# Windowed attention with channel mix on one core: the converted weights' bits in PSUM between VectorE's operations, and eight in place of six blocks begun in seven slots

## The chip, the cores and the metric

One core of one Trainium2 chip. The metric is the device time of one execution in microseconds (us); the median of three runs stands for the kernel.

## The reference

Attention with a window of 96 keys and 8 global keys, a bias that falls with distance, and a gated channel mix of its output with the output of the token before:

```python
scores = q @ k.T / 8 + bias, masked            # B = 4, H = 8, S = 768, D = 64
x = (softmax(scores) @ v) as [4, 768, 512]
x_prev = x shifted by one token
xk = mu_k * x + (1 - mu_k) * x_prev
xr = mu_r * x + (1 - mu_r) * x_prev
k = max(xk @ w_k, 0)                           # w_k: 512 x 1024
out = sigmoid(xr @ w_r) * ((k * k) @ w_v)      # w_r: 512 x 512, w_v: 1024 x 512
```

q, k and v are float32, the three weights float64; the output is float32.

## The kernel before

**Tiles and chunks.** The 3072 queries are 24 tiles of 128 (6 for each batch), each with all 8 heads. For a tile, `scores` makes four products s (two heads each), VectorE adds the bias and takes the row maximum (e, L295), ScalarE takes the exponent (L296), VectorE the reciprocal of the sums of four heads (r, L302 and L303), and GpSimd scales the four heads' e by it (L306). `transposes` turns e on TensorE (t, L317) and ScalarE copies it (et, L318). `weighted` makes the products av with v (L334). Two tiles are a chunk of 256 tokens, x, and twelve chunks go through the channel mix: `mix` (GpSimd's or ScalarE's product and VectorE's L358, then hi and lo parts, xk_lo and xr_lo at L360), four products kp of 24 matmuls (L371 to L373 in `three`), their squares kk (L397 to L400), two products z of 12, two products vps of 24, and the output sig. The first seven tiles (NATIVE) multiply plain float32; from tile 7 on queries and keys are split into two float32r parts (qh, ql, kw; L265 and L266).

**Weights.** The float64 weights are 20 blocks of 128x512: 0 to 7 of w_k, 8 to 11 of w_r, 12 to 19 of w_v. `weight_begin` loads block i's words (raw, in the profile w or w64_i; 512 KB), ScalarE takes the high word's absolute value into a (in the profile wa), and a range step follows: for i < 8 on GpSimd (L167), for later blocks on VectorE (L170). Three operations of VectorE put the float32's bits together: shift and mask (L171), sign (L172), low word (L173). ScalarE or GpSimd rounds a to the hi part (L196 is GpSimd's), and `weight_end` subtracts on GpSimd for the lo part (L180). In all VectorE does 3 operations for each of blocks 0 to 7 and 4 for each of the others, 72.

**Buffers.** Blocks 0 to 7 lie in the buffers of the channel mix (f_pool); raw of the others takes one of three buffers t4k, which mixes and raw queries and keys use too; a of the others one of four f2. In PSUM there are eight banks: two for s, two for t, one for av, and three with the tag "f", which the idle products at the start, kp, z and vps share. A buffer of a tag is taken again when the last reader of the tile before it is done.

**What sets the order.** The main loop calls, for each tile and each of its four pairs of heads, the transposes and scores, then `run_ffn` for pieces of an earlier chunk's channel mix (a chunk begins LAG = 3 tiles after its first tile), then `weights_go`, which begins blocks up to a number n of the slot. On top of that the framework's scheduler orders the instructions of each engine by a model of their times, so the order on an engine need not be that of the code, and a changed line can reorder others. The order is fixed when the kernel is built. Each engine works through its own list; SyncE issues the loads in order, each waiting for its buffer.

Of the kernel before, what the change touches and what calls it, by code (L numbers as in the profile page):

```python
# [9 lines left out]
F32 = mybir.dt.float32  # L10
F32R = mybir.dt.float32r
BF16 = mybir.dt.bfloat16
I32 = mybir.dt.int32
U32 = mybir.dt.uint32
AF = mybir.ActivationFunctionType
ALU = mybir.AluOpType
# [3 lines left out]
B, H, S, D = 4, 8, 768, 64  # L20
# [3 lines left out]
NCHUNK = NTILES // 2  # L24
NATIVE = 7  # first tiles, whose scores are plain float32 products
GMAX = 32
LMAX = 97
NEG = -1.0e9
FAR = 1.0e12
HUGE = (1.875 - 2.0**-13) * 2.0**32  # bits 0x4FEFFC00  # L30


@with_exitstack
def tile_biased_attention_channel_mix(ctx: ExitStack, tc: tile.TileContext, qT, kT, v, n_sizes, mu_kr, w_k, w_v, w_r, q_rows, k_rows, v_rows, slopes, out):
    nc = tc.nc
    vec, act, pool, pe = nc.vector, nc.scalar, nc.gpsimd, nc.tensor

    const = ctx.enter_context(tc.tile_pool(name="const", bufs=1))

# [1 line left out]
    sizes_w = const.tile([128, 2, 2], I32, name="sizes_w")  # L41
    nc.sync.dma_start(sizes_w.rearrange("p s w -> p (s w)"), n_sizes.partition_broadcast(128))
    words = const.tile([128, 2, 2], F32, name="words")
    sizes = const.tile([128, 2], F32, name="sizes")
# [15 lines left out]

# [1 line left out]
    wts = {}  # L62
# [17 lines left out]
    ps_f = fast.enter_context(tc.tile_pool(name="ps_f", bufs=3, space=PSUM))  # L80

    # the tensor engine's clock rises with use: products of zeros until the first tile is there
    zeros = const.tile([128, 512], BF16, name="zeros")
# [4 lines left out]

# [1 line left out]
    # The distance; n_local for a key that is only global, which is over any distance of a local key;  # L90
    # FAR or more where masked: such a key's weight is exactly 0.
    pat = const.tile([128, H, 256], BF16, name="pat")
# [9 lines left out]
    ints, flts, local, glo, dist0, dist = (piece() for _ in range(6))  # L102
    ints = ints.bitcast(I32)
    j = flts[:, 224:352]
    # 96 keys before the tile, then the tile's own
    pool.iota(ints[:, 96:224], [[-1, 128]], base=0, channel_multiplier=1)
# [7 lines left out]

    # tile 0
    vec.tensor_scalar(local[:, 96:224], causal, nlf, FAR, op0=ALU.is_ge, op1=ALU.mult)
# [9 lines left out]

    # later tiles: 32 keys from the start, 96 keys before the tile, the tile
    vec.tensor_scalar(local[:, 0:96], flts[:, 0:96], nlf, FAR, op0=ALU.is_ge, op1=ALU.mult)
# [15 lines left out]
    def weight_begin(i):  # L144
        # A float64 weight's words: (sign, 11 exponent bits, 20 bits), (32 bits).
        # a: its first 24 significant bits as a float32; hi: a rounded to float32r; lo: the rest of a.
        name, src, k, c = w_steps[i]
        if name != "k":
            raw = p4k.tile([128, 512, 2], I32, tag="t4k", name=f"w64_{i}")
            a = f2_pool.tile([128, 512], I32, tag="f2", name=f"wa_{i}")  # L150
        elif k < 2:
            both = f_pool.tile([128, 2048], I32, tag=("kk_hi", "kk_lo")[k], name=f"w64_{i}")
            raw = both[:, 0:1024].rearrange("p (n w) -> p n w", w=2)
            a = both[:, 1024:1536]
        else:
            t = "xk" if k == 2 else "xr"
            raw = f_pool.tile([128, 512, 2], I32, tag=t + "_hi", name=f"w64_{i}")
            a = f_pool.tile([128, 512], I32, tag=t + "_lo", name=f"wa_{i}")
        nc.sync.dma_start(raw.rearrange("p n w -> p (n w)"), src[k * 128 : (k + 1) * 128, 2 * c : 2 * c + 1024])
        low, top = raw[:, :, 0], raw[:, :, 1]  # L160
        hi = wts[name][0][:, k, c : c + 512]
        # top's bits as a float32: times 2**-112 (or 2**16, which differs in a bit that the shift drops) moves the float64
        # exponent's bias to the float32's. What float32 cannot hold is bounded: from 2**128 up (by Inf, which stays Inf,
        # or the min) to a large number, under 2**-127 (by underflow or the max) to 0.
        if i < 8:
            act.activation(a.bitcast(F32), top.bitcast(F32), AF.Abs, scale=2.0**111)
            pool.tensor_scalar(a.bitcast(F32), a.bitcast(F32), 2.0**-112, 2.0**-111, op0=ALU.mult, op1=ALU.mult)  # L167
        else:
            act.activation(a.bitcast(F32), top.bitcast(F32), AF.Abs, scale=2.0**16)
            vec.tensor_scalar(a.bitcast(F32), a.bitcast(F32), 2.0, HUGE, op0=ALU.max, op1=ALU.min)  # L170
        vec.tensor_scalar(a, a, 3, 0x7FFFFFF8, op0=ALU.logical_shift_left, op1=ALU.bitwise_and)  # L171
        vec.scalar_tensor_tensor(a, top, -0x80000000, a, op0=ALU.bitwise_and, op1=ALU.bitwise_or)  # L172
        vec.scalar_tensor_tensor(a, low, 29, a, op0=ALU.logical_shift_right, op1=ALU.bitwise_or)  # L173
        (act.copy if i % 4 < 2 else pool_copy)(hi, a.bitcast(F32))
        w_live[i] = a
# [21 lines left out]

# [1 line left out]
    state = {}  # L199
    # the first tiles' queries and keys, with 64 rows of zeros: products of all 128 rows keep the tensor engine's clock up  # L200
    padded = []
# [40 lines left out]
    def global_v(n):  # L242
        # the tile before, now with the 32 first rows in place of its own
        b, t = divmod(n, NT)
        if t >= 2:
            nc.sync.dma_start(state[n - 1]["va"][0:32], v[b, 0:32, :])
# [99 lines left out]

# [1 line left out]
    def mix(xc, xp, tag, tmp_pool, out_pool, on_act=False):  # L348
# [73 lines left out]

# [1 line left out]
    LAG = 3  # tiles from a chunk's first to the start of its channel mix  # L424
    queue = []
# [15 lines left out]
    for step in range(NTILES + 1):  # L441
        if step + 1 < NTILES:
            load_tile(step + 1)
        if step < NTILES:
            load_v(step)
        for hp in range(4):
            if hp == 0 and step > 1:
                for i in range(4):
                    weighted(step - 2, i)
                global_v(step - 1)  # L450
            if step:
                transposes(step - 1, hp)
            if step < NTILES:
                scores(step, hp)
            if hp == 0:
                if step >= LAG and (step - LAG) % 2 == 0:
                    queue.append(ffn((step - LAG) // 2))
                    if len(queue) == 1 and step == LAG:
                        budget[0] = -17.5
            run_ffn(2.5)  # L460
            run_ffn(2.5)
            if hp == 1 and step + 1 < NTILES:
                split_tile(step + 1)
            slot = 4 * step + hp
            n = min(8, 2 + slot * 4 // 3) if slot < 6 else 8 + (slot - 5) * 6 // 7
            weights_go(n, n - 1 if n <= len(w_steps) else n)
# [7 lines left out]

# [1 line left out]
    def wide():  # L476
        with ExitStack() as g:
# [5 lines left out]
            ps_f = g.enter_context(tc.tile_pool(name="g_psf", bufs=3, space=PSUM))  # L483
            xs = dram.tile([B * DM, S], F32, name="xs")

            dist, keep = ([once.tile([128, S], F32, name=f"{n}_{t}") for t in range(NT)] for n in ("dist", "keep"))
# [9 lines left out]
            for t in range(NT):  # L496
                pool.iota(ji, [[-1, S]], base=t * 128, channel_multiplier=1)
                vec.tensor_copy(rel, ji)
                loc = keep[t]
                vec.tensor_scalar(loc, rel, 0.0, None, op0=ALU.is_ge)  # L500
                vec.tensor_scalar(tmp, rel, nlf, None, op0=ALU.is_lt)
                vec.tensor_mul(loc, loc, tmp)
                # only global: n_local; else the distance
                vec.tensor_sub(tmp, glob, loc)
                vec.tensor_scalar(tmp, tmp, 0.0, None, op0=ALU.max)
                vec.tensor_scalar(keep_n, tmp, nlf, None, op0=ALU.mult)
                vec.tensor_scalar(tmp, tmp, -1.0, 1.0, op0=ALU.mult, op1=ALU.add)
                vec.scalar_tensor_tensor(dist[t], rel, -1.0, rel, op0=ALU.mult, op1=ALU.max)
                vec.tensor_mul(dist[t], dist[t], tmp)
                vec.tensor_add(dist[t], dist[t], keep_n)  # L510
                vec.tensor_max(keep[t], loc, glob)
# [68 lines left out]

    # 1 where the short windows do not hold every kept key
    okf = const.tile([128, 2], F32, name="okf")
# [56 lines left out]
```

## Time and profile before

| | |
|---|---|
| median of 3 runs | 526.06 us (525.92 to 526.25) |
| the profiled execution: span, and with what lies around it | 524.1 us, 526.06 us at the median |
| TensorE busy | 495.9 us, 95% of the span |
| VectorE busy | 372.4 us, 71% |
| ScalarE busy | 323.6 us, 62% |
| GpSimd busy | 283.0 us, 54% |
| chain that ended last | PE 80%, DVE 11%, POOL 5% |
| page's TensorE clock | 0.7 to 0.9 of full in parts of the first 65 us, full behind |

PE is TensorE (PEld its weight loads), DVE VectorE, ACT ScalarE, POOL GpSimd, SP SyncE. L12 is line 12 of the kernel. In a row of a timeline the first number is the start, the second the duration in us (from the first's start to the last's end where several are joined: x4); "out<-in" names tiles without their numbers. An instruction's duration can overlap the next one on its engine by its start-up, so the distance of two starts is what an instruction costs in a row of them. Shares over the whole span mix the start-up, in which weights are converted, with the long stretch behind it.

### The profile page before, as it was taken

How to read it: one execution, taken by the hardware profiler on the slowest of the kernel's cores; microseconds unless marked ns; L12 is line 12 of the kernel's file. 1: busy time of each engine (PE TensorE's matmuls, PEld its weight loads, DVE VectorE, ACT ScalarE, POOL GpSimd, SP SyncE). 2: the span in 40 equal slices, each digit the busy share in tenths (PEclk: the TensorE clock that was granted, in tenths of full speed). 3: DMA queues.
4: the chain of work that ended last, by engine and by line, in shares of the span. 5: the costliest groups of instructions: out<-in, count | busy, mean ns of one | idle time of the engine just before them, and what ended most of it. 6: DMA issues, size and time to landing. Idle time of an engine off the chain costs nothing.

```text
span 524.1 us, 9900 instructions
## 1 busy us (share of the span) xinstructions
PE 495.9 (95%) x3466; PEld 427.2 (82%) x3466; DVE 372.4 (71%) x854; ACT 323.6 (62%) x730; POOL 283.0 (54%) x410
## 2 busy tenths in 40 slices
PE   7885888979999999999999999999999999999995
PEld 4563766869898898898898898898898898898984
DVE  6799999987677766767767867767777865535321
ACT  4868585823957856846847757756757667643220
POOL 8799977987355644544547645535547634203000
PEclk9979799999999999999999999999999999999999
DMA  8998268150350530530521431521422210000101
GB/s 197 322 232 198 67 185 188 41 144 20 107 134 6 141 107 5 157 91 8 162 76 38 130 86 34 133 86 59 124 62 66 62 46 26 35 12 2 41 1 44
DMA packets 27304, 48.16 MB, mean 92 GB/s; under 512 B 7216, under 2 KB 13360, under 8 KB 27248
## 3 DMA queue, kind: packets, MB, share of 16 engines
q1 hardware_dynamic: 27104, 47.46, 34.0%
q8 instruction: 29, 0.48, 0.4%
q14 instruction: 27, 0.22, 0.1%
q10 hardware_dynamic: 144, 0.00, 0.0%
HBM read 41.16 MB, written 6.29 MB: 91 GB/s over the span
## 4 chain that ended last, share of the span: by engine, by line
PE 80%; DVE 11%; POOL 5%; issue 3%; DMA 1%; ACT 0%; DVEq 0%; POOLq 0%
PE vps L372 8%; PE vps L373 8%; PE vps L371 8%; PE kp L371 8%; PE kp L373 8%; PE kp L372 8%; PE av L334 7%; PE t L317 6%; PE z L371 4%; PE z L373 4%; PE z L372 4%; PE s L290 3%; PE s L289 3%; POOL e L306 2%; PE s L287 2%
## 5 line engine op out<-in xcount | busy, mean ns | idle before, releaser
L306 POOL TENSOR_SCALAR e<-e,r 128x256 f32<-128x256 f32 (+1 forms) x192 | 106.1, 570 | 137.0 <-DVE r L303 91.9
L371 PE MATMUL kp<-xk_hi,wk_hi 128*128 128x256 f32 x384 | 108.0, 282 | 0.2 <-DVE kk L398 0.2
L373 PE MATMUL kp<-xk_hi,wk_lo 128*128 128x256 f32 x384 | 107.5, 280 | 0.5 <-POOL wk_lo L180 0.5
L372 PE MATMUL kp<-xk_lo,wk_hi 128*128 128x256 f32 x384 | 107.3, 279 | 0.0
L296 ACT ACTIVATE e<-e,nmax 128x256 f32<-128x256 f32 (+1 forms) x192 | 92.6, 484 | 22.0 <-DVE nmax L295 21.0
L295 DVE CUSTOM_DVE_ANT_0 e<-s,pat 128x256 f32<-128x256 f32 (+1 forms) x192 | 69.0, 395 | 31.0 <-PE s L290 21.2
L372 PE MATMUL vps<-wv_lo,kk_hi 128*128 128x512 f32 x192 | 76.0, 396 | 2.6 <-POOL wv_lo L180 2.6
L371 PE MATMUL vps<-wv_hi,kk_hi 128*128 128x512 f32 x192 | 75.9, 395 | 0.4 <-POOL wv_hi L196 0.4
L373 PE MATMUL vps<-wv_hi,kk_lo 128*128 128x512 f32 x192 | 75.8, 395 | 0.0
L371 PEld LDWEIGHTS kp<-xk_hi,wk_hi 128*128 128x128 f32 x384 | 72.9, 190 | 1.2 <-DVE kk L398 0.6
L373 PEld LDWEIGHTS kp<-xk_hi,wk_lo 128*128 128x128 f32 x384 | 72.8, 190 | 0.9 <-POOL wk_lo L180 0.9
L372 PEld LDWEIGHTS kp<-xk_lo,wk_hi 128*128 128x128 f32 x384 | 72.9, 190 | 0.6
L318 ACT COPY et<-t 128x512 f32<-128x512 f32 (+1 forms) x96 | 52.0, 546 | 20.2 <-PE t L317 19.7
L317 PE MATMUL t<-ident,e 128*128 128x128 f32 x352 | 57.5, 280 | 5.7 <-POOL e L306 5.6
L398 DVE TENSOR_TENSOR kk<-kp,kk 128x512 f32<-128x512 f32 x48 | 33.1, 689 | 41.2 <-ACT kk L397 41.0
L317 PEld LDWEIGHTS t<-ident,e 128*128 128x128 f32 x352 | 41.2, 141 | 19.1 <-POOL e L306 9.2
L334 PE MATMUL av<-et,va 128*64 128x128 f32 x704 | 49.4, 284 | 0.6 <-ACT et L318 0.6
L334 PEld LDWEIGHTS av<-et,va 128*64 128x64 f32 x704 | 40.3, 139 | 10.5 <-issue 5.8
L400 DVE TENSOR_TENSOR kk_lo<-kk,kk_hi 128x512 fp32r<-128x512 f32 x48 | 35.3, 735 | 17.4 <-ACT kk_hi L399 17.3
L399 ACT CAST kk_hi<-kk 128x512 fp32r<-128x512 f32 x48 | 29.8, 622 | 25.6 <-DVE kk L398 25.6
L397 ACT ACTIVATE kk<-kp 128x512 f32<-128x512 f32 x48 | 28.3, 590 | 26.7 <-PE kp L373 24.5
L372 PEld LDWEIGHTS vps<-wv_lo,kk_hi 128*128 128x128 f32 x192 | 36.0, 187 | 10.5 <-POOL wv_lo L180 3.1
(103 smaller groups left out, 1051.1 us busy)
## 6 DMA issues: line engine op xcount, KB each, us to landing
kraw<-in_kT_dram SPq DMA_DIRECT2D x36, 256.0 KB, 3.9
qraw<-in_qT_dram SPq DMA_DIRECT2D x34, 256.0 KB, 4.1
va<-in_v_dram SPq DMA_DIRECT2D x24, 256.0 KB, 3.1
out_dram<-sig SPq DMA_DIRECT2D x24, 256.0 KB, 3.5
w<-in_w_k_dram SPq DMA_DIRECT2D x8, 512.0 KB, 9.1
w<-in_w_v_dram SPq DMA_DIRECT2D x8, 512.0 KB, 3.5
kz<-in_kT_dram SPq DMA_DIRECT2D x8, 256.0 KB, 6.7
w<-in_w_r_dram SPq DMA_DIRECT2D x4, 512.0 KB, 9.3
```

What stands on the lines that cost most here:

```text
L295: vec.tensor_tensor_reduce(out=e[:, :w], in0=o, in1=p[:, h, :], op0=ALU.add, op1=ALU.min, scale=-0.125, scalar=3.0e38, accum_out=s["nmax"] ...
L296: act.activation(e[:, :w], e[:, :w], AF.Exp, bias=s["nmax"][:, h : h + 1], scale=-1.0, accum_out=s["sum"][:, h : h + 1])
L306: pool.tensor_scalar(e[:, :w], e[:, :w], r[:, u : u + 1], 1.0, op0=ALU.mult, op1=ALU.mult)
L317: pe.transpose(pt[:, c : c + 128], e[:, k * 128 : (k + 1) * 128], ident)
L318: act.copy(et[:, : 2 * nb * 128], pt[:, : 2 * nb * 128])
L334: pe.matmul(o, vt[:, h * 64 : (h + 1) * 64], et[:, c : c + 128], start=k == 0, stop=k == nb - 1)
L371: pe.matmul(o, sh, mh, start=first, stop=False)
L372: pe.matmul(o, sh, ml, start=False, stop=False)
L373: pe.matmul(o, sl, mh, start=False, stop=last)
L398: vec.tensor_mul(kk, pv, kk)
L399: act.copy(kkh[:, 2 * fp : 2 * fp + 2, :], kk)
L400: vec.tensor_sub(kkl[:, 2 * fp : 2 * fp + 2, :], kk, kkh[:, 2 * fp : 2 * fp + 2, :])
```

## The change

The bits of block i get a tile of their own in PSUM, wb_i, with the tag "f". The range step of the later blocks (L170) writes there, the shift (L171) and the sign (L172) read and write there, and the low word's operation (L173) reads it and writes a in SBUF as before. From slot 6 on, blocks are begun at a rate of 8 in 7 slots, not 6 in 7. One line is added, so from L162 on every line of the code before has a number higher by one in the changed kernel. Comments are taken out, which moves nothing.

```diff
         hi = wts[name][0][:, k, c : c + 512]
+        bits = ps_f.tile([128, 512], I32, name=f"wb_{i}", tag="f")
         if i < 8:
             act.activation(a.bitcast(F32), top.bitcast(F32), AF.Abs, scale=2.0**111)
             pool.tensor_scalar(a.bitcast(F32), a.bitcast(F32), 2.0**-112, 2.0**-111, op0=ALU.mult, op1=ALU.mult)
         else:
             act.activation(a.bitcast(F32), top.bitcast(F32), AF.Abs, scale=2.0**16)
-            vec.tensor_scalar(a.bitcast(F32), a.bitcast(F32), 2.0, HUGE, op0=ALU.max, op1=ALU.min)
-        vec.tensor_scalar(a, a, 3, 0x7FFFFFF8, op0=ALU.logical_shift_left, op1=ALU.bitwise_and)
-        vec.scalar_tensor_tensor(a, top, -0x80000000, a, op0=ALU.bitwise_and, op1=ALU.bitwise_or)
-        vec.scalar_tensor_tensor(a, low, 29, a, op0=ALU.logical_shift_right, op1=ALU.bitwise_or)
+            vec.tensor_scalar(bits.bitcast(F32), a.bitcast(F32), 2.0, HUGE, op0=ALU.max, op1=ALU.min)
+        vec.tensor_scalar(bits, a if i < 8 else bits, 3, 0x7FFFFFF8, op0=ALU.logical_shift_left, op1=ALU.bitwise_and)
+        vec.scalar_tensor_tensor(bits, top, -0x80000000, bits, op0=ALU.bitwise_and, op1=ALU.bitwise_or)
+        vec.scalar_tensor_tensor(a, low, 29, bits, op0=ALU.logical_shift_right, op1=ALU.bitwise_or)
...
             slot = 4 * step + hp
-            n = min(8, 2 + slot * 4 // 3) if slot < 6 else 8 + (slot - 5) * 6 // 7
+            n = min(8, 2 + slot * 4 // 3) if slot < 6 else 8 + (slot - 5) * 8 // 7
```

The scheduler answers with another order. In the rows below an instruction has its line, its operation, what it writes and reads with the tiles' numbers, and its size; t_3_0 is tile 3's first transpose, kp_700 and kp_748 are chunk 0's first product in the one and the other kernel, mix_k and xk_lo of chunk 0 are its mixes.

TensorE, before: where chunk 0's products begin, among the transposes of tile 3.

```order
L334 MATMUL av_2_729<-et_2_3_676,va_2_413 64x128
L317 MATMUL t_3_0_750<-ident_62,e_3_0_582 128x128 x2
L371 MATMUL kp_700<-xk_hi_589,wk_hi_70 128x256
L371 MATMUL kp_783<-xk_hi_589,wk_hi_70 128x256
L317 MATMUL t_3_0_750<-ident_62,e_3_1_585 128x128 x2
L317 MATMUL t_3_1_812<-ident_62,e_3_2_634 128x128 x2
L317 MATMUL t_3_1_812<-ident_62,e_3_3_637 128x128 x2
L372 MATMUL kp_700<-xk_lo_590,wk_hi_70 128x256
```

TensorE, after: where chunk 0's products begin.

```order
L335 MATMUL av_5_1480<-et_5_3_1433,va_5_1021 64x128
L318 MATMUL t_6_3_1642<-ident_62,e_6_6_1442 128x128
L318 MATMUL t_6_3_1642<-ident_62,e_6_7_1445 128x128
L335 MATMUL av_6_1699<-et_6_0_1499,va_6_1234 64x128 x2
L335 MATMUL av_6_1699<-et_6_1_1560,va_6_1234 64x128 x2
L335 MATMUL av_6_1699<-et_6_2_1609,va_6_1234 64x128 x2
L335 MATMUL av_6_1699<-et_6_3_1643,va_6_1234 64x128 x2
L372 MATMUL kp_748<-xk_hi_613,wk_hi_70 128x256
L373 MATMUL kp_748<-xk_lo_614,wk_hi_70 128x256
```

Before, chunk 0's first products stand between two transposes of tile 3, and tiles 4 to 6 follow among the rest of them. After, all transposes and all products av of tiles 0 to 6 stand first, and chunk 0's four kp, two z and two vps follow in one piece with chunk 1's behind them.

VectorE, before: the place where chunk 0's mix is made.

```order
L171 TENSOR_SCALAR wa_6_322<-wa_6_322 128x512
L172 SCALAR_TENSOR_TENSOR wa_6_322<-w64_6_321,wa_6_322 128x512
L358 SCALAR_TENSOR_TENSOR mix_k_588<-x_0_424,mus_67,mix_k_588 128x256
L295 ISA e_3_6_685,nmax_3_477<-s_3_3_682,pat_140 128x256
L295 ISA nmax_3_477 128x1
L295 ISA e_3_7_688,nmax_3_477<-s_3_3_682,pat_140 128x256
L295 ISA nmax_3_477 128x1
L358 SCALAR_TENSOR_TENSOR mix_k_588<-x_0_424,mus_67,mix_k_588 128x256
L173 SCALAR_TENSOR_TENSOR wa_6_322<-w64_6_321,wa_6_322 128x512
L171 TENSOR_SCALAR w64_5_291<-w64_5_291 128x512
L358 SCALAR_TENSOR_TENSOR mix_k_588<-x_0_424,mus_67,mix_k_588 128x256 x2
```

VectorE, after: the rows around the end of tile 6's row maxima (e_6_6 and e_6_7 are tile 6's last heads, r_6_3 its last reciprocals).

```order
L296 ISA e_6_6_1442,nmax_6_1142<-s_6_3_1439,pat0_141 128x128
L296 ISA nmax_6_1142 128x1
L171 TENSOR_SCALAR wb_11_502<-wa_11_500 128x512
L296 ISA e_6_7_1445,nmax_6_1142<-s_6_3_1439,pat0_141 128x128
L296 ISA nmax_6_1142 128x1
L172 TENSOR_SCALAR wb_11_502<-wb_11_502 128x512
L171 TENSOR_SCALAR wb_12_529<-wa_12_527 128x512
L173 SCALAR_TENSOR_TENSOR wb_11_502<-w64_11_499,wb_11_502 128x512
L303 TENSOR_SCALAR r_6_3_1448<-sum_6_1141 128x4
L172 TENSOR_SCALAR wb_12_529<-wb_12_529 128x512
L174 SCALAR_TENSOR_TENSOR wa_11_500<-w64_11_499,wb_11_502 128x512
L304 RECIPROCAL r_6_3_1448<-r_6_3_1448 128x4
```

VectorE, after: the end of the stretch from there to the operation for which kp_748 waits, the last row here (its buffer is that of wb_15).

```order
L361 TENSOR_TENSOR xk_lo_614<-mix_k_612,xk_hi_613 128x1024
L361 TENSOR_TENSOR xr_lo_627<-mix_r_625,xr_hi_626 128x1024
L171 TENSOR_SCALAR wb_14_641<-wa_14_639 128x512
L172 TENSOR_SCALAR wb_14_641<-wb_14_641 128x512
L173 SCALAR_TENSOR_TENSOR wb_14_641<-w64_14_638,wb_14_641 128x512
L171 TENSOR_SCALAR wb_15_651<-wa_15_649 128x512
L174 SCALAR_TENSOR_TENSOR wa_14_639<-w64_14_638,wb_14_641 128x512
L172 TENSOR_SCALAR wb_15_651<-wb_15_651 128x512
L171 TENSOR_SCALAR wb_16_688<-wa_16_686 128x512
L173 SCALAR_TENSOR_TENSOR wb_15_651<-w64_15_648,wb_15_651 128x512
L172 TENSOR_SCALAR wb_16_688<-wb_16_688 128x512
L174 SCALAR_TENSOR_TENSOR wa_15_649<-w64_15_648,wb_15_651 128x512
```

Before, chunk 0's mix stands among row maxima of tiles 3 and 4 and operations of blocks 5 and 6. After, it stands with blocks 11 to 13 behind e_6_6, and blocks 14 to 16 follow it. Between the two pieces shown stand the rest of blocks 12 and 13, kw_7 and the eight mixes of chunk 0; blocks 0 to 10 lie ahead, among tiles 2 to 6.

SyncE, before: the loads around kraw_7.

```order
L159 DMA w64_13_614<-in_w_v_dram 128x1024
L223 DMA qz_0_177<-in_qT_dram 64x1024
L226 DMA kz_0_178<-in_kT_dram 64x8x128
L159 DMA w64_14_665<-in_w_v_dram 128x1024
L239 DMA va_5_1000<-in_v_dram 128x512
L159 DMA w64_15_713<-in_w_v_dram 128x1024
L246 DMA va_3_551<-in_v_dram 32x512
L159 DMA w64_16_802<-in_w_v_dram 128x1024
L159 DMA w64_17_873<-in_w_v_dram 128x1024
L226 DMA kraw_7_1207<-in_kT_dram 64x8x128
L228 DMA kraw_7_1207<-in_kT_dram 64x8x128
```

SyncE, after: the loads around va_6.

```order
L229 DMA kraw_7_1227<-in_kT_dram 64x8x128
L240 DMA va_6_1234<-in_v_dram 128x512
L247 DMA va_4_776<-in_v_dram 32x512
L159 DMA w64_11_499<-in_w_r_dram 128x1024
L159 DMA w64_12_526<-in_w_v_dram 128x1024
L159 DMA w64_13_560<-in_w_v_dram 128x1024
L159 DMA w64_14_638<-in_w_v_dram 128x1024
L159 DMA w64_15_648<-in_w_v_dram 128x1024
L159 DMA w64_16_685<-in_w_v_dram 128x1024
L159 DMA w64_17_712<-in_w_v_dram 128x1024
```

Before, the loads of blocks 13 to 17 stand ahead of kraw_7, between the tiles' loads. After, blocks 11 to 19 stand behind kraw_7 (whose four loads are the rows ahead of these) and va_6.

## The prediction

> **What bounds the kernel now.** I read the stretches of the span first, because a kernel with a start-up stage has no single bound. The columns are busy time and (x) instructions of each engine, granted TensorE clock, DMA share and GB/s.
>
> ```profile
> core 0: us, PE busy (x) PEld busy (x) DVE busy (x) ACT busy (x) POOL busy (x), PEclk, DMA share, GB/s
> 0.00:26.00 26.00, 20.41 (x88) 12.99 (x88) 18.44 (x85) 16.71 (x54) 20.45 (x38) 1.00 0.99 261
> 26.00:69.00 43.00, 33.30 (x211) 25.70 (x212) 41.48 (x88) 28.69 (x75) 39.29 (x42) 0.84 0.70 157
> 69.00:112.00 43.00, 36.60 (x233) 29.32 (x234) 41.50 (x91) 28.36 (x68) 37.08 (x42) 1.00 0.55 146
> 134.00:518.00 384.00, 384.00 (x2784) 340.39 (x2784) 253.67 (x571) 240.80 (x520) 172.93 (x278) 1.00 0.25 68
> ```
>
> From 134 us TensorE is busy without a gap; nothing that the change does to VectorE can shorten that. From 26 to 112 us VectorE is busy 83 of 86 us and GpSimd 76, while TensorE has holes. The change touches weight blocks, which all lie before 112 us. So the question is one number: when does TensorE reach the point from which its order is the same in both kernels? That point, P below, is the first matmul of chunk 1's vps, at 133.60 us. Then the waits, for who is late in the start-up (us in total, times, longest):
>
> ```profile
> ACT et L318 <- PE t L317: 9.6, 7, 3.2
> POOL e L306 <- DVE r L303: 6.6, 3, 3.8
> PE s L287 <- DVE nmax L295: 5.8, 2, 3.2
> PE t L317 <- POOL e L306: 4.6, 9, 1.2
> ```
>
> Attention is a ring here: VectorE's row maximum, exponent, VectorE's reciprocal, GpSimd's scaling (L306), TensorE's transposes (L317), and the transposes free the buffers of the next tile. No wait is long, because each engine has weight work or channel mix to fill its gaps. Third, what the weights cost VectorE, grouped by form:
>
> ```profile
> L173 DVE SCALAR_TENSOR_TENSOR wa<-w,wa 128x512 int32<-128x512 int32 x16 | 15.1, 948 | 0.0
> L172 DVE SCALAR_TENSOR_TENSOR wa<-w,wa 128x512 int32<-128x512 int32 x16 | 12.6, 795 | 0.1
> L170 DVE TENSOR_SCALAR wa<-wa 128x512 f32<-128x512 f32 x12 | 10.4, 874 | 0.0
> L171 DVE TENSOR_SCALAR wa<-wa 128x512 int32<-128x512 int32 x16 | 8.5, 535 | 0.0
> L171 DVE TENSOR_SCALAR w<-w 128x512 int32<-128x512 int32 x4 | 3.3, 820 | 1.0 <-POOL w L167 1.0
> L173 DVE SCALAR_TENSOR_TENSOR w<-w 128x512 int32<-128x512 int32 x4 | 2.9, 734 | 0.0
> L172 DVE SCALAR_TENSOR_TENSOR w<-w 128x512 int32<-128x512 int32 x4 | 2.7, 682 | 0.0
> ```
>
> 72 instructions, 55.5 us, .77 each. The same instruction varies much:
>
> ```profile
> 70.24 0.42 DVE L170 TENSOR_SCALAR wa<-wa 128x512 f32<-128x512 f32 x1
> 70.55 0.44 DVE L295 CUSTOM_DVE_ANT_0 e<-s,pat 128x256 f32<-128x256 f32 x1
> ...
> 75.85 1.52 DVE L170 TENSOR_SCALAR wa<-wa 128x512 f32<-128x512 f32 x1
> ...
> 89.54 0.68 DVE L398 TENSOR_TENSOR kk<-kp,kk 128x512 f32<-128x512 f32 x1
> 90.14 0.68 DVE L172 SCALAR_TENSOR_TENSOR wa<-w,wa 128x512 int32<-128x512 int32 x1
> 90.74 0.17 DVE L303 RECIPROCAL r<-r 128x4 f32<-128x4 f32 x1
> ```
>
> L170 took .31 from its start to the next at 70.24, and 1.52 at 75.85, beside GpSimd. Over the whole span, min/median/max ns:
>
> ```profile
> L398 DVE TENSOR_TENSOR kk<-kp,kk x8: 673/678/684, 81.7 to 130.3; 128x512 f32<-128x512 f32 x8
> ...
> L400 DVE TENSOR_TENSOR kk_lo<-kk,kk_hi x8: 662/692/1784, 84.9 to 131.7; 128x512 fp32r<-128x512 f32 x8
> ```
>
> L398, with one input in PSUM (kp) and one in SBUF, is never stretched (684 at most up to 134 us); L400, with both in SBUF, is, to 1784.
>
> **The price of one changed operation.** The trace has no bitwise operation on PSUM. Bounds: .31 (L170 undisturbed in SBUF) and .95 (the mean of L173). I take .60, the start-to-start of L398 at 89.54, the nearest row: same shape, one PSUM and one SBUF operand. For the two stt (L172, L173) that is what they take in SBUF undisturbed (90.14 to 90.74); for the two tensor_scalar (L170, L171) it is twice the undisturbed .31. The Trainium skill, page "VectorE: DVE Perf Modes", section "Why PSUM operands drop a tier", says that a PSUM operand holds fp32 work at the single rate; that speaks against the change for these 32 instructions, and L398's .60 beside L170's .31 agrees. If they kept .31 instead, the sum below would be 3.5 us less (12 of them on the decisive path). So all 72 would cost 43.2 us, 12.3 less than now, and GpSimd should be less disturbed.
>
> **The order decides what that is worth.** Before, chunk 0's mix and first products lie among tiles 3 to 6, and blocks fill VectorE's gaps between the tiles. After, the blocks' bits take buffers of the same pool as kp, z and vps (tag "f", three of them), and all of chunk 0's products stand behind the last product of tile 6; the first kp takes the buffer that block 15's bits leave. VectorE reaches block 15's last operation only behind the last row maximum but one of tile 6 (e_6_6), 22 weight operations, kw_7, eight mix operations and two lo parts. So I count the time T1 at which block 15 is done.
>
> Rows for the sum; GpSimd first:
>
> ```profile
> 20.85 3.85 POOL L306 TENSOR_SCALAR e<-e,r 128x256 f32<-128x256 f32 x4 [1.82 <-DVE r L303]
> 24.67 1.28 POOL L180 TENSOR_TENSOR wk_lo<-w,wk_hi 128x512 fp32r<-128x512 f32 x1
> 25.92 0.62 POOL L167 TENSOR_SCALAR w<-w 128x512 f32<-128x512 f32 x1
> ...
> 34.12 3.80 POOL L306 TENSOR_SCALAR e<-e,r 128x256 f32<-128x256 f32 x4
> ...
> 42.03 2.44 POOL L306 TENSOR_SCALAR e<-e,r 128x256 f32<-128x256 f32 x4
> ```
>
> Four scalings take 3.80 beside VectorE's SBUF work and 2.44 undisturbed. The Trainium skill, "SBUF — State Buffer", section "Who interferes with whom", says that VectorE with at most one SBUF input and outside its two-port modes leaves GpSimd alone, and with two SBUF inputs does not; L398 against L400 agrees. By it GpSimd would gain what I give it next.
>
> Stage A, to block 0's first operation on VectorE: tile 1's scalings start as now at 20.85, two undisturbed quads (4.88) and one L167 (.62): 26.4. Stage B: blocks 0 and 1, three operations each at .60, and two row maxima and a reciprocal (1.0) stand ahead of tile 2's first scaling: 31.0 (now 34.12). From there GpSimd's queue up to e_5_4, all at undisturbed prices: 7 quads (17.1), 9 lo parts at 1.30 (11.7; 1.28 above), 5 hi parts (3.1) and 4 L167 (2.5) at .62 (a hi part is the same single-input copy of 128x512), and one small copy of x, taken like them at .6: 35.0. So 66.0, and I add 1.8 for a wait on a late reciprocal (half of the longest, 3.8, that the waits show) and .7 for the transposes that release e_6_6: 68.5. VectorE has only about 28 us of work in that stretch; the blocks that could fill the rest stand behind e_6_6. That is the step on which the forecast rests: the relief of VectorE finds no work to take it.
>
> Stage C, on VectorE alone:
>
> ```profile
> 98.06 0.69 DVE L358 SCALAR_TENSOR_TENSOR mix_k<-x,mus,mix_k 128x256 f32<-128x256 f32 x1
> ...
> 104.34 1.21 DVE L360 TENSOR_TENSOR xk_lo<-mix_k,xk_hi 128x1024 fp32r<-128x1024 f32 x1
> ...
> 120.44 2.35 DVE L266 TENSOR_TENSOR kw<-kraw,kw 64x2048 fp32r<-64x2048 f32 x1
> ```
>
> 22 weight operations at .60 (13.2), kw_7 2.35, 8 mixes at .69 (5.5), two lo parts (2.5), a row maximum and reciprocals (.5): 24.0. SyncE issues w_11 to w_17 behind kraw_7 and va_6, and each of them waits for an earlier block's buffer; the loads land in
>
> ```profile
> w<-in_w_v_dram SPq DMA_DIRECT2D x8, 512.0 KB, 3.5
> ...
> w<-in_w_r_dram SPq DMA_DIRECT2D x4, 512.0 KB, 9.3
> ```
>
> so that VectorE gets ahead of them once or twice; bounds 0 and 6 (w_11's nine less three that are covered), taken 2. T1 = 68.5 + 26.0 = 94.5.
>
> Stage D, TensorE from T1 to P. Its rates:
>
> ```profile
> 61.30 0.40 PE L373 MATMUL kp<-xk_hi,wk_lo 128*128 128x256 f32 x1
> 61.51 0.30 PE L371 MATMUL kp<-xk_hi,wk_hi 128*128 128x256 f32 x1
> ...
> 62.24 0.28 PE L372 MATMUL kp<-xk_lo,wk_hi 128*128 128x256 f32 x1
> 62.36 0.28 PE L373 MATMUL kp<-xk_hi,wk_lo 128*128 128x256 f32 x1
> ...
> 133.60 0.39 PE L371 MATMUL vps<-wv_hi,kk_hi 128*128 128x512 f32 x1
> 133.83 0.39 PE L372 MATMUL vps<-wv_lo,kk_hi 128*128 128x512 f32 x1
> ```
>
> kp every .12 us (62.24 to 62.36), .21 while the clock is low after idling (61.30 to 61.51), vps and z every .23. Chunks 0 and 1 have 192 kp (22.6), 48 z (11.2) and chunk 0 48 vps (11.2), .5 for tile 7's first scores: 45.5. Added: the clock after 20 us of idling, 1.7 (18 kp at .09 more); a wait of the third kp product for block 18's last operation, 3.5 (it stands 17 rows behind block 15's on VectorE, 11 at .60, the rest mixes and kk's at .60 to .69: 10.7; the two products ahead take 7.2 with the slow clock); a wait of vps for the last kk, which stands behind ql_7 and its load, 1.3 (an estimate; bounds 0 and 3.5, a load of such a size). Together 52.0: P = 146.5. Against 133.60 now, where 6 transposes and 8 products of tile 6 (1.1) are still to come: **+11.8**. I take 11 as the forecast, because the two last waits can overlap with the slow clock: the profiled execution's 524.1 us would become 535.1; 1.96 us lie around its span at the median (526.06), so **537.0**. The three runs lie within .33 us, so the execution is taken for one of them.
>
> For nothing go: moving L170 to L173 of blocks 0 to 7 (already in the sum), ScalarE (28 busy of 43 in both stretches above) and DMA bandwidth (share .55 to .70). Where ScalarE became late, wa's abs, it would delay the blocks in stage C, inside its 0 to 6.
>
> **Rivals.**
> *B, the order as above, but dearer.* PSUM operations at .80 (towards the .95), and GpSimd still disturbed, quads at 3.1 between 2.44 and 3.80: 22 × .20 = 4.4, 7 × .66 = 4.6, so 9 us more: 546. For it: L173's mean .948 has two SBUF inputs, and low lies in SBUF still. Against: L398's narrow spread.
> *C, faster: VectorE's work alone sets T1.* It is a matter of stage B: if its gaps were filled, T1 would be the sum of VectorE's work. To 112 us that is now 101.4 us, by the three stretches above. Less 14 operations of blocks 16 to 19 that T1 doesn't wait for (10.8), chunk 0's kk and kk_lo (8 × .7), chunk 1's mix and lo parts (8.2), plus kw_7 and the rest of tile 6 (3), less 58 × (.77 − .60) = 9.9: 69.9, and 10.6 of idling as now: T1 = 80.5, P = 132.5 against 134.7, so 524. It decides from T1 below 82.7 on. That section of the Trainium skill's "SBUF — State Buffer", with the conflicts gone and nothing else in the way, leads here too. Against it: GpSimd's queue to e_5_4 is 35 us even undisturbed, and stands ahead of e_6_6.
> *D, no change:* T1 between 81.6 and 83.6, by stages B and C each 6 us shorter than counted: 526.
> *The change does nothing:* excluded by the order; the forecast is that it does too much to the order.
>
> **How the numbers follow.** A, the forecast, .60, own range 530 to 543: stage C by its lower bound (ts at .31, no wait for loads: −5.5) and B's start ±3 make the lower end, +6 (loads 4, late reciprocals 2) the upper. B .20 (543 to 551), C .14 (515 to 525), D .06. The range 525 to 548 leaves out C and B's upper part, 2 in 10 at most. A change of .2% (1 us) is about what a measurement can tell. A and B are slower, .80, of which .01 is left to no change, so same .07; C is faster, .14.
>
> **What would show it.** Right: TensorE idle for over 15 us between tile 6's last product and the first kp, released by VectorE's last operation of a block; that first kp at 90 to 99 us; L171 to L173 (a line later then) at .60 to .70 with little spread; quads of L306 at 2.5 in stage B; P at 142 to 149, and the same 384 us behind it. Wrong: the first kp before 83, or weight operations on PSUM over .9. If e_6_6 comes much before 68, GpSimd's queue was mis-sized, and C gains.

## The result, and the profile after

The changed kernel takes 541.46 us (median of 4 runs, 541.07 to 541.60) against 526.15 us: 15.3 us slower, ratio 1.0289 (95% interval 1.0275 to 1.0304). The forecast was 537.0. The stretches of the profiled execution (span 539.6 us), with the columns as before:

```profile
core 0: us, PE busy (x) PEld busy (x) DVE busy (x) ACT busy (x) POOL busy (x), PEclk, DMA share, GB/s
0.00:26.00 26.00, 19.40 (x94) 13.13 (x94) 14.91 (x81) 16.90 (x57) 18.41 (x41) 0.93 0.99 260
26.00:69.00 43.00, 36.00 (x257) 26.05 (x256) 35.13 (x118) 33.84 (x101) 30.62 (x50) 0.92 0.87 192
69.00:112.00 43.00, 22.37 (x130) 18.86 (x131) 39.89 (x62) 19.12 (x39) 31.10 (x36) 0.58 0.30 99
...
146.00:534.00 388.00, 388.00 (x2788) 343.52 (x2786) 251.12 (x565) 240.63 (x517) 168.49 (x270) 1.00 0.24 67
```

VectorE and GpSimd have less to do up to 69 us than before (50 and 49 us busy, not 60 and 60). What has grown is the idle time of TensorE from 69 to 112 us: 22.4 us busy, not 36.6, and that at a granted clock of .58. Behind 146 us it is busy without a gap, as it was. The weight operations of VectorE:

```profile
L173 DVE SCALAR_TENSOR_TENSOR wb<-w,wb 128x512 int32<-128x512 int32 x20 | 13.5, 687 | 0.1
L174 DVE SCALAR_TENSOR_TENSOR wa<-w,wb 128x512 int32<-128x512 int32 x16 | 10.7, 677 | 0.1
L172 DVE TENSOR_SCALAR wb<-wb 128x512 int32<-128x512 int32 x12 | 8.2, 690 | 0.0
L171 DVE TENSOR_SCALAR wb<-wa 128x512 f32<-128x512 f32 x12 | 8.2, 688 | 2.8 <-ACT wa L170 2.6
L172 DVE TENSOR_SCALAR wb<-wa 128x512 int32<-128x512 int32 x4 | 2.6, 684 | 0.0
L172 DVE TENSOR_SCALAR wb<-w 128x512 int32<-128x512 int32 x4 | 2.6, 684 | 0.0
L174 DVE SCALAR_TENSOR_TENSOR w<-w,wb 128x512 int32<-128x512 int32 x4 | 2.6, 678 | 0.0
```

Every one takes .68 to .69, 48.4 us in all against 55.5. The operands did what the change says; the 15 us come from elsewhere. TensorE at the first kp before, and then around it in the changed kernel (a number in brackets is idle time and its releaser):

```profile
54.79 0.48 PE L371 MATMUL kp<-xk_hi,wk_hi 128*128 128x256 f32 x2
```

```profile
87.70 3.74 PE L335 MATMUL av<-et,va 128*64 128x128 f32 x32 [8.14 <-ACT x L346]
...
94.06 1.98 PE L335 MATMUL av<-et,va 128*64 128x128 f32 x16 [2.01 <-ACT x L346]
96.10 0.58 PE L372 MATMUL kp<-xk_hi,wk_hi 128*128 128x256 f32 x1
96.48 0.41 PE L373 MATMUL kp<-xk_lo,wk_hi 128*128 128x256 f32 x1
...
100.05 0.28 PE L372 MATMUL kp<-xk_hi,wk_hi 128*128 128x256 f32 x1
100.17 0.28 PE L373 MATMUL kp<-xk_lo,wk_hi 128*128 128x256 f32 x1
...
107.59 0.58 PE L372 MATMUL kp<-xk_hi,wk_hi 128*128 128x256 f32 x1 [3.85 <-DVE wa L174]
...
113.30 0.41 PE L374 MATMUL kp<-xk_hi,wk_lo 128*128 128x256 f32 x1
...
113.69 0.28 PE L373 MATMUL kp<-xk_lo,wk_hi 128*128 128x256 f32 x1
...
151.08 0.39 PE L372 MATMUL vps<-wv_hi,kk_hi 128*128 128x512 f32 x1
```

The first kp starts at 96.10 (before: 54.79), the third waits 3.85 us for a block's last operation, and the point P, before at 133.60, is at 151.08. The shift of 17.5 is 2.0 us more than that of the spans (15.5): tile 6's rest, which stood behind P before and took about 1.4 us there, stands ahead of it now. The other .6 is not accounted for.

### The profile page after: what moved, and what is told of

It reads as the page before. It is cut to its first block, busy times and chain, and to the rows that moved or that the text cites. A ratio compares the mean times of both kernels' runs of the same rounds, so it can differ in the third digit from the quotient of the medians.

```text
span 539.6 us, 9929 instructions
## 1 busy us (share of the span) xinstructions
PE 499.3 (93%) x3466; PEld 431.3 (80%) x3466; DVE 361.9 (67%) x854; ACT 321.9 (60%) x728; POOL 260.7 (48%) x410
## 4 chain that ended last, share of the span: by engine, by line
PE 76%; DMA 8%; DVE 8%; ACT 3%; POOL 2%; issue 2%; SPq 1%; DVEq 0%; POOLq 0%; ACTq 0%
PE vps L374 8%; PE vps L372 8%; PE vps L373 8%; PE kp L372 7%; PE kp L374 7%; PE kp L373 7%; PE t L318 6%; PE av L335 6%; PE z L372 4%; PE z L374 4%; PE z L373 4%; PE s L291 3%; PE s L290 3%; DMA w<-in_w_v_dram 3%; DMA kz<-in_kT_dram 2%
## 5 line engine op out<-in xcount | busy, mean ns | idle before, releaser
L307 POOL TENSOR_SCALAR e<-e,r 128x256 f32<-128x256 f32 (+1 forms) x192 | 90.1, 488 | 154.8 <-DVE r L304 110.7
L372 PE MATMUL kp<-xk_hi,wk_hi 128*128 128x256 f32 x384 | 109.7, 286 | 4.5 <-DVE wa L174 3.8
L374 PE MATMUL kp<-xk_hi,wk_lo 128*128 128x256 f32 x384 | 108.6, 283 | 0.0
L373 PE MATMUL kp<-xk_lo,wk_hi 128*128 128x256 f32 x384 | 108.6, 283 | 0.0
L372 PEld LDWEIGHTS kp<-xk_hi,wk_hi 128*128 128x128 f32 x384 | 74.4, 194 | 5.8 <-DVE wa L174 4.5
L373 PEld LDWEIGHTS kp<-xk_lo,wk_hi 128*128 128x128 f32 x384 | 74.3, 194 | 0.5
L374 PEld LDWEIGHTS kp<-xk_hi,wk_lo 128*128 128x128 f32 x384 | 74.2, 193 | 0.0
L318 PE MATMUL t<-ident,e 128*128 128x128 f32 x352 | 59.4, 287 | 9.7 <-POOL e L307 9.6
L335 PE MATMUL av<-et,va 128*64 128x128 f32 x704 | 50.2, 289 | 12.3 <-ACT x L346 10.2
L401 DVE TENSOR_TENSOR kk_lo<-kk,kk_hi 128x512 fp32r<-128x512 f32 x48 | 34.1, 710 | 18.7 <-ACT kk_hi L400 18.7
L374 PEld LDWEIGHTS vps<-wv_hi,kk_lo 128*128 128x128 f32 x192 | 36.0, 187 | 8.9
```

What stands on the lines that cost most here:

```text
L307: pool.tensor_scalar(e[:, :w], e[:, :w], r[:, u : u + 1], 1.0, op0=ALU.mult, op1=ALU.mult)
L318: pe.transpose(pt[:, c : c + 128], e[:, k * 128 : (k + 1) * 128], ident)
L335: pe.matmul(o, vt[:, h * 64 : (h + 1) * 64], et[:, c : c + 128], start=k == 0, stop=k == nb - 1)
L372: pe.matmul(o, sh, mh, start=first, stop=False)
L373: pe.matmul(o, sh, ml, start=False, stop=False)
L374: pe.matmul(o, sl, mh, start=False, stop=last)
```

## The experiments

The theory was the prediction's: the order of the queues costs the time, and the operations themselves save some. Against it stood the price of the PSUM operands, the waits of kp for the blocks' buffers, and the rate of beginning. Each kernel was timed beside the kernel before, whose median was 525.91 to 526.64 us there. xk_lo is the start of chunk 0's xk_lo, z that of its first z, both from the profiles.

| kernel | bits in PSUM | blocks begun | order in which blocks are begun | xk_lo | z | median, us | ratio (95% interval) |
|---|---|---|---|---|---|---|---|
| before | none | 6 in 7 | 0 to 19 | 55.3 | 90.3 | 526.15 | 1 |
| changed | all | 8 in 7 | 0 to 19 | 86.0 | 116.0 | 541.46 | 1.0289 (1.0275, 1.0304) |
| e1 | all | 6 in 7 | 0 to 19 | 80.2 | 106.5 | 535.51 | 1.0170 (1.0146, 1.0194) |
| e2 | none | 8 in 7 | 0 to 19 | 75.3 | 110.5 | 539.91 | 1.0260 (1.0242, 1.0277) |
| e3 | none | | all queues as changed | 92.1 | 115.5 | 548.68 | 1.0434 (1.0413, 1.0454) |
| e4 | 0 to 7 | 6 in 7 | 0 to 19 | 68.5 | 89.1 | 526.15 | .9998 (.9989, 1.0008) |
| e5 | none | | all queues as e4 | 71.7 | 92.6 | 529.84 | 1.0075 (1.0058, 1.0092) |
| e6 | all | 5 in 7 | 1 2 3 0 8 9 10 6 5 7 11 4 12 ... | 56.9 | 84.7 | 527.09 | 1.0022 (1.0010, 1.0034) |
| e7 | all | 6 in 7 | as e6 | 61.0 | 95.1 | 524.06 | .9951 (.9934, .9967) |
| e8 | all | 8 in 7 | as e6 | 70.2 | 110.7 | 534.39 | 1.0167 (1.0127, 1.0208) |
| e9 | none | | all queues as e7 | 63.5 | 99.3 | 535.91 | 1.0174 (1.0156, 1.0192) |
| e10 | all, own bank | 8 in 7 | 0 to 19 | 82.9 | 112.3 | 554.16 | 1.0533 (1.0513, 1.0552) |
| e11 | 8 to 19 | 6 in 7 | 0 to 19 | 58.1 | 96.7 | 529.66 | 1.0050 (1.0032, 1.0069) |
| e12 | all | 5 in 7 | as e6, mix first | 58.9 | 90.0 | 534.28 | 1.0153 (1.0135, 1.0170) |

**The order and the operands apart: e3.** VectorE's lines of the kernel before, with 8 in 7, and every engine's instructions tied to the changed kernel's order, by edges that set the order of issue and wait for nothing (the list of numbers is left out here):

```diff
+def pin(tc):
+    traced = list(tc.nc.cur_bb.bb.instructions)
...
+        for x, y in zip(order, order[1:]):
+            tc.add_manual_dep(mine[y], mine[x].name, info, reason="pin")
```

> VectorE's weight operations of the kernel before, with the bits in SBUF, but every engine's instructions issued in exactly the order of the changed kernel. Theory (order): as slow as the changed kernel, 537 to 547 us, with first kp at 92 to 103 us, since loads and the queue set it, not the price of an operation. Rival (PSUM operands make the operations or their chain dear): 526 to 531 us.

548.68 us. In the two profiles the instructions of TensorE, VectorE, ScalarE and GpSimd follow each other in the same order. The order alone costs 22.7 us over the kernel before (526.0 beside it), and PSUM operands in the same order give 7.2 back (541.46). The price of PSUM operands is ruled out as the cause. That the edges themselves cost nothing was not measured: there is no run of the changed kernel tied to its own order. The measured time is over the range given, by 1.7; VectorE's sign and low-word operations took .94 and .97 there (L195 and L196; the written-out order moves all lines), but that this is the 1.7 isn't shown:

```profile
L196 DVE SCALAR_TENSOR_TENSOR wa<-w,wa 128x512 int32<-128x512 int32 x16 | 15.4, 973 | 0.0
L195 DVE SCALAR_TENSOR_TENSOR wa<-w,wa 128x512 int32<-128x512 int32 x16 | 15.0, 939 | 0.1
```

**One half of the change at a time: e1 and e2.**

```diff
-            n = min(8, 2 + slot * 4 // 3) if slot < 6 else 8 + (slot - 5) * 8 // 7
+            n = min(8, 2 + slot * 4 // 3) if slot < 6 else 8 + (slot - 5) * 6 // 7
```

is e1, made to the changed kernel; the reverse, made to the kernel before, is e2.

> The changed kernel with the rate put back: bits in PSUM, 6 blocks begun in 7 slots. Theory (the order of the queues costs the time, and sharing tag f with PSUM bits brings that order): here too all row maxima and transposes of tiles 0 to 6 stand ahead of chunk 0's first kp, so 535 to 545 us, first kp at 88 to 100 us. Rival (the rate of 8 in 7 crowds VectorE): back to 524 to 528 us.

> The kernel before with the rate alone: bits in SBUF, 8 blocks begun in 7 slots. Chunk 0's first kp stand between the transposes of tile 4, half a tile to a tile later than before. Theory (order): a small loss, 525 to 531 us. Rival (the rate is the cause): 537 to 543 us.

e1 went as the theory had it, 9.5 us slower. e2 went the rival's way: the rate alone costs 13.9 us in SBUF. Its operations are those of the kernel before, so it, too, can only cost by the order: chunk 0's mix stands behind more blocks (48 weight operations ahead of xk_lo on VectorE, 34 before), and its z comes 20 us later,

```profile
110.48 0.80 PE L371 MATMUL z<-wr_hi,xr_hi 128*128 128x512 f32 x1 [5.43 <-DVE kk L398]
```

So either half alone spoils the order, and the two do not add (9.5 and 13.9 against 15.3 together). The prediction had not told them apart.

**Why PSUM bits change the order: e6, e7 and e8.** In the kernel before VectorE finishes the blocks as 1 2 3 0 8 9 10 6 5 7 11 4 12 and so on: 8 to 10 fill gaps while 4 to 7 wait for the mix's buffers, which 0 to 3 hold. In the changed kernel it finishes them strictly as 0 to 19, in the order in which the code asks for a buffer with the tag "f". These three ask in the order of the kernel before:

```diff
+ORDER = [1, 2, 3, 0, 8, 9, 10, 6, 5, 7, 11, 4, 12, 13, 14, 15, 16, 17, 18, 19]
...
-            weight_begin(w_count[0])
+            weight_begin(ORDER[w_count[0]])
...
-            weight_end(w_count[1])
+            weight_end(ORDER[w_count[1]])
```

> The same with 6 blocks in 7 slots; chunk 0's first kp stand among tile 4's transposes. Theory: 516 to 527 us, the later start of chunk 0 eating part of what the cheaper operations save. Rival (sharing): 530 to 540 us.

> The same with the changed kernel's 8 blocks in 7 slots; chunk 0's first kp stand behind tile 5's transposes. Theory (the rate, too, acts by putting blocks ahead of chunk 0's mix): 526 to 536 us, between the slower rate and the changed kernel. Rival (block order alone was at fault): 514 to 523 us.

> The changed kernel (all bits in PSUM) with the blocks begun in the order 1 2 3 0 8 9 10 6 5 7 11 4 12 to 19, which is the order in which VectorE finishes them in the kernel before, and 5 in 7 slots. Theory (PSUM buffers are given out in the order of the code, so blocks 8 to 10 could not fill VectorE's early gaps and chunk 0 came late; the operations themselves are cheaper): chunk 0's first kp at 55 to 70 us and 514 to 523 us. Rival (sharing tag f with kp, z and vps costs the time in any order): 530 to 540 us.

With the rates of e1 and of the changed kernel, the block order alone is worth 11.5 and 7.1 us. e7, 524.06 us, is the only kernel that beats both. It scatters (522.78 to 528.21), and its profiled execution is the slowest of its five. Sharing the tag with kp, z and vps need not cost the time: e6 and e7 do it. e6, at 527.09, missed both its ranges; it started chunk 0 earlier than e7 and gained nothing. Its w_v blocks come late, and TensorE waits for them within 105 to 150 us, which it doesn't in e7:

```profile
PE vps L375 <- POOL wv_lo L182: 3.3, 2, 2.4
```

**What the operands are worth in better orders: e4, e5 and e9.** e4 puts only the first blocks' bits in PSUM,

```diff
-        bits = ps_f.tile([128, 512], I32, name=f"wb_{i}", tag="f")
+        bits = ps_f.tile([128, 512], I32, name=f"wb_{i}", tag="f") if i < 8 else a
```

with 6 in 7; e5 and e9 are the orders of e4 and e7 with SBUF bits, tied as in e3.

> Bits in PSUM for the first 8 blocks only, 6 blocks begun in 7 slots; chunk 0's first kp stand between the transposes of tile 3, as before the change. Theory (order costs, the PSUM operations themselves save some .1 us each on VectorE and free GpSimd): 518 to 527 us, weight operations on PSUM at .68 to .70 us with little spread. Rival (PSUM bits cost time wherever they stand): 528 to 535 us.

> Bits in SBUF throughout, every engine's instructions issued in exactly the order of the kernel with PSUM bits for the first 8 blocks. It shows what the operands alone are worth in an order that starts chunk 0 early. Theory (PSUM operands save time in any order, 7 us for 72 operations in the changed kernel's): 24 operations, so 527 to 531 us, 1 to 5 above its PSUM twin. Rival (they are worth nothing where the chain runs through other engines): within 1 us of it, 525 to 527 us.

> Bits in SBUF, every engine's instructions in exactly the order of the kernel with PSUM bits, the block order 1 2 3 0 8 9 10 6 5 7 and 6 in 7 slots (524.06 us). It shows whether that kernel's gain is the operands' or the order's. Theory (operands are worth some 7 us for 72 operations, as in the changed kernel's order): 528 to 534 us. Rival (the gain comes from the order): 522 to 526 us.

In equal orders PSUM saves 3.7 us for 24 operations (e5 less e4), 11.9 for 72 (e9 less e7; e9 is 1.9 over its range, and the two profiled executions, e7's its slowest, differ by 7.8) and 7.2 for 72 (e3 less the changed kernel). The weight operations of VectorE themselves got shorter by nothing (54.1 us in e5, 54.4 in e4), 4.6 (53.0 and 48.4) and 7.4 (55.8 and 48.4). So in the first two pairs more was saved than VectorE's operations give. GpSimd got faster as well, which can be the rest; no run parts the two. Its scaling of e from 26 to 112 us, first e7, then e9:

```profile
L309 POOL TENSOR_SCALAR e<-e,r 128x256 f32<-128x256 f32 x34 | 18.4, 561 | 4.1 <-DVE r L306 4.1
```

```profile
L332 POOL TENSOR_SCALAR e<-e,r 128x256 f32<-128x256 f32 x36 | 29.2, 830 | 1.1 <-DVE r L329 1.1
```

and the changed kernel against e3, which has its order:

```profile
L307 POOL TENSOR_SCALAR e<-e,r 128x256 f32<-128x256 f32 x32 | 14.7, 478 | 8.1 <-DVE r L304 8.1
```

```profile
L329 POOL TENSOR_SCALAR e<-e,r 128x256 f32<-128x256 f32 x32 | 23.0, 733 | 5.1 <-DVE r L326 5.1
```

**Own bank: e10.**

```diff
-    ps_f = fast.enter_context(tc.tile_pool(name="ps_f", bufs=3, space=PSUM))
+    ps_f = fast.enter_context(tc.tile_pool(name="ps_f", bufs=2, space=PSUM))
+    ps_w = fast.enter_context(tc.tile_pool(name="ps_w", bufs=1, space=PSUM))
...
-        bits = ps_f.tile([128, 512], I32, name=f"wb_{i}", tag="f")
+        bits = ps_w.tile([128, 512], I32, name=f"wb_{i}", tag="wb")
```

> The changed kernel, with the bits in one PSUM bank of their own and two banks left for kp, z and vps, so that no kp waits for a block's buffer. The blocks still go in the order 0 to 19 and all transposes up to tile 6 stand ahead of chunk 0. Theory (buffers given out in the order of the code set the queues' order, the sharing itself costs little): 536 to 546 us. Rival (the waits of kp for block 15's and 18's buffers cost the time): 526 to 532 us.

554.16 us, over what either side gave. No kp waits for a block any more, here as in e3, and both are slower than the changed kernel, so those waits were not what made it slow. But with two banks a kp waits for kk, and the first still waits for the mix:

```profile
82.76 0.80 PE L373 MATMUL kp<-xk_hi,wk_hi 128*128 128x256 f32 x2 [10.64 <-ACT xk_hi L361]
...
103.54 0.58 PE L373 MATMUL kp<-xk_hi,wk_hi 128*128 128x256 f32 x1 [7.28 <-DVE kk L400]
```

**Two more tries: e11** (as e4 with `if i >= 8`) **and e12** (e6, with `tc.high_priority()` around chunk 0's mix).

> Bits in PSUM for blocks 8 to 19 only (48 of the 72 operations), 6 in 7 slots; blocks 0 to 7 have no PSUM buffers to wait for and go as in the kernel before, chunk 0's first kp among tile 4's transposes. Theory: near the kernel with the block order and 6 in 7, 521 to 528 us. Rival (blocks 8 to 19 in tag f are what makes the changed kernel slow): 532 to 540 us.

> All bits in PSUM, the block order, 5 in 7 slots, and chunk 0's mix given priority in the scheduler. A try for a faster kernel: chunk 0's first kp stand behind the first product of tile 4. Theory: between the 5-in-7 and the 6-in-7 kernel or under both, 519 to 527 us. Rival (no lever left in that order, ScalarE and loads set the pace): 525 to 530 us.

Both missed. e11 is near its range (529.66), and blocks 8 to 19 in the tag are not, by themselves and at 6 in 7, what makes the changed kernel slow. e12 lost 7.2 us to e6 with chunk 0's mix hardly moved (xk_lo 58.9 and 56.9) and its z 5.3 us later. In its profile tile 6's exponents and qraw_7's load come behind chunk 0's first sigmoid at 93 to 116 us; why the priority did that, and whether it is all of it, was not settled. Nor do the two columns settle a time: e4 and e12 begin z within 1 us of each other and lie 8.1 us apart. That the order costs the time is shown; what each piece of it costs is read from the profiles.

## Why the prediction was right, point by point

**The order (right).** Chunk 0's products stand behind all of tile 6 and blocks up to 15, and that costs more than the operands save, as forecast: 15.3 us, where the sum had 11. With the old operands the same order costs 22.7 (e3). The 4.5 us that the forecast lacks are 1.5 in T1, 3.0 in stage D and the .8 that was taken off, less .9, since 2.0 us, and not 1.1, moved from behind P to ahead of it.

**The price of an operation (right).** .60 from start to start was taken, and these three rows, in which two blocks take turns, show .61 and .59 (the three operations of one block just ahead of them took .73 to .80):

```profile
91.20 0.69 DVE L171 TENSOR_SCALAR wb<-wa 128x512 f32<-128x512 f32 x1
91.81 0.68 DVE L174 SCALAR_TENSOR_TENSOR wa<-w,wb 128x512 int32<-128x512 int32 x1
92.40 0.69 DVE L172 TENSOR_SCALAR wb<-wb 128x512 int32<-128x512 int32 x1
```

The shift and range operations went from the undisturbed .31 to .60. The Trainium skill, "VectorE: DVE Perf Modes", "Why PSUM operands drop a tier", says that a PSUM operand holds fp32 work at the single rate; these rows agree.

**Stages A and B (right in time, wrong in what fills them).** Tile 2's first scaling was put at 31.0, e_6_6 at 68.5:

```profile
30.39 1.84 POOL L307 TENSOR_SCALAR e<-e,r 128x256 f32<-128x256 f32 x4 [5.50 <-DVE r L304]
```

```profile
69.07 0.29 DVE L296 CUSTOM_DVE_ANT_0 e<-s,pat 128x128 f32<-128x128 f32 x1 [0.86 <-PE t L318]
...
95.36 0.68 DVE L174 SCALAR_TENSOR_TENSOR wa<-w,wb 128x512 int32<-128x512 int32 x1
```

But four scalings take 1.84, not the 2.44 that was called undisturbed. With that GpSimd's queue, put at 35.0, held 29.6 us of work. Its waits, put at 1.8, came to 8.0: 2.6 for reciprocals, and 5.4 for hi parts that ScalarE makes:

```profile
56.42 1.28 POOL L181 TENSOR_TENSOR wk_lo<-w,wk_hi 128x512 fp32r<-128x512 f32 x1 [4.30 <-ACT wk_hi L175]
...
66.10 1.28 POOL L181 TENSOR_TENSOR wr_lo<-wa,wr_hi 128x512 fp32r<-128x512 f32 x1 [1.07 <-ACT wr_hi L175]
```

So the stretch filled up with what the sum priced at nothing: ScalarE, 33.8 of 43 us busy and not 28.7, and loads. The chain of waits of this kernel has there, among exponents and ScalarE's work on blocks,

```profile
22.23 10.10 DMA kz<-in_kT_dram
...
65.35 5.36 DMA w<-in_w_v_dram
```

Two errors cancelled, and that is luck: the scalings were priced too high, and ScalarE and DMA bandwidth, which were to go for nothing, were not free.

**Stage C (right in time, with a second path that was not seen).** 26.0 was taken from e_6_6 to block 15's end; 69.07 to 96.04 are 27.0. The first kp is at 96.10, forecast 94.5, but block 15 isn't all that ends there: tile 6's products av end at 96.04 too, after 10.2 us of waits for ScalarE's copy into x, and kp follows them without idle time. That copy follows xr_hi on ScalarE, and GpSimd's copy into the same x waits for the last mix_r: chunk 0's mix, late, holds back tile 5 as well. e3 shows that this second path is enough. There the bits lie in SBUF, no kp waits for a block, and the first still stands right behind tile 6's products:

```profile
99.73 1.98 PE L357 MATMUL av<-et,va 128*64 128x128 f32 x16 [1.56 <-ACT x L368]
101.64 0.58 PE L394 MATMUL kp<-xk_hi,wk_hi 128*128 128x256 f32 x1
```

That is 9.5 us behind xk_lo, in the changed kernel 10.1. When block 15 alone would have let the first kp start, without this path, stays open.

**Stage D (a term missing).** 52.0 was taken from T1 to P, measured 55.0. The work is the 45.5 that was counted. Two of the other terms are there: the third kp's wait, 3.85 for 3.5, and the slow clock at the start, 18 kp at .21 up to 99.9. No row of the prediction gives the 18, and as far as these rows show it is luck: 2.0 us of tile 6's products, which it did not expect there, ran right ahead of them. vps did not wait for a kk, which was put at 1.3; in its place a kp of chunk 1 waited .59 at 136.66 for the bank that chunk 0's vps left. Missing is that the clock falls again in the third kp's wait:

```profile
87.00:96.00 9.00, 6.29 (x50) 5.20 (x50) 7.83 (x13) 4.06 (x10) 4.47 (x4) 0.50 0.69 234
96.00:100.00 4.00, 3.94 (x20) 3.90 (x19) 3.83 (x7) 1.26 (x2) 3.22 (x3) 0.50 0.80 259
100.00:107.50 7.50, 3.75 (x32) 3.54 (x31) 6.57 (x13) 3.36 (x6) 3.28 (x5) 0.95 0.09 37
107.50:112.00 4.50, 4.41 (x20) 4.41 (x21) 4.50 (x7) 0.62 (x1) 4.29 (x6) 0.50 0.01 2
```

.50 again from 107.5, and kp at .21 up to 113.5: 28 of them take 6.1 us, at full rate 3.3, so 2.8 more. With it D is whole: by the distances of starts, 45.5, 1.8 for the first slow clock, 4.0 for the wait, 2.8 and .8 for chunk 1's kp are 54.9. And the step from +11.8 to 11, because the waits could overlap with the slow clock, went the wrong way: here a wait brought the slow clock back.

**The rivals.** B (dearer operations, GpSimd still disturbed) is out by the rows: .69 and 1.84. C (VectorE's work alone sets T1) is out, since T1 is 96 and not 80.5; with the block order put right, e7 shows what of its gain there is, 1.9 us (525.91 beside it).

**The signs.** Three came true: the first kp at 90 to 99, the operations at .60 to .70, and a stretch behind P without a gap. Three did not: TensorE was not idle between tile 6's last product and the first kp (over 15 us expected; its idle time lies ahead of those products), four scalings took 1.84 and not 2.5, and P, at 151.08, lies behind the 142 to 149 that were given.

## What to carry to other kernels

A change that makes operations cheaper can change the order of the whole program where buffers come from a shared pool and a scheduler orders the queues: read the order of each engine around the first consumer before counting microseconds. New operations that take buffers in the order of the code lose the freedom to pass each other; ask for the buffers in the order in which the data is ready. To part the two effects, run the old operations in the new order: here it split the loss of some 15 us into +22.7 and −7.2.

## What the runs showed of the hardware

GpSimd's scaling of 128x256 takes .48 and .56 us with VectorE's bits in PSUM (the changed kernel and e7) and .73 and .83 in the same orders with bits in SBUF (e3 and e9). The Trainium skill, "SBUF — State Buffer", "Who interferes with whom", says that a VectorE instruction with two SBUF inputs contends with GpSimd's reads, and one with at most one, outside the two-port modes, doesn't; this agrees. In two of three pairs with equal orders, more time was saved than VectorE's operations got shorter by.

TensorE's granted clock fell to .50 in a wait of only 3.85 us and came back 5.9 us into unbroken kp (107.6 to 113.5). After the long idle stretch it came back 5.8 us into unbroken work, av from 94.06 and kp behind it up to 99.9; the work from 87.70 to 92.05, with a gap of 2.0 behind it, had not brought it back (.50 over 87 to 96). The Trainium skill, "TensorE: Matmul & The Clock Gate", "HAM oscillation — how this bites in real kernels", gives gaps of over about 3.4 us as what brings the half clock back; this wait agrees. From the last kp ahead of the wait, at 103.47, to 113.69 are 10.2 us, where kp at full rate take 3.4. So a wait of 4 us cost 6.8.
